# Eight expert token lists, 512-row matmul blocks, and output rows summed by gather and scatter in a linear-attention and mixture-of-experts kernel

## The chip, the cores and the metric

One NeuronCore of a Trainium2 chip. The metric is the device time of one execution in microseconds (us). The kernel before takes 836.64 us (median of 3 runs, 836.46 to 836.75). The engines are named as in the profile: PE is TensorE (PEld its weight loads), DVE is VectorE, ACT is ScalarE, POOL is GpSimd, SP is SyncE.

## The reference, cut to what matters

```python
def _attn_ref(q, k, v):                       # 8 batches, 8 heads, 576 tokens, 64 wide
    phi = lambda x: np.where(x > 0, x, np.exp(x) - 1.0) + 1.0
    kv  = np.einsum('bhsd,bhse->bhde', phi(k), v)
    num = np.einsum('bhsd,bhde->bhse', phi(q), kv)
    den = np.einsum('bhsd,bhd->bhs', phi(q), phi(k).sum(axis=2))[..., None] + 1e-06
    return num / den                          # 4608 token rows x of 512

def _moe_ref(x, w_gate, w_noise, noise, w1, w2):   # 8 experts, 512 -> 1024 -> 512
    noisy = x @ w_gate + np.log1p(np.exp(x @ w_noise)) * noise
    # the two largest per token and their softmax: top2, top2_w
    for e in range(8):
        for k in range(2):
            mask = top2[:, k] == e
            h = np.maximum(x[mask] @ w1[e], 0.0)
            out[mask] += top2_w[mask, k, None] * (h @ w2[e])
```

Every token goes through two experts, so 9216 rows run through the expert matmuls and every output row is the sum of two.

## The kernel before

Three stages follow one another. **Attention and routing** works through 40 tiles of up to 128 tokens. Each tile is routed by itself, with small VectorE operations on 128 x 8 elements, and scattered twice, into one sorted list per choice slot (first or second choice) and expert:

```python
    for b in range(B):
        # ... phi(q), phi(k), k-v products of the batch ...
        for ci in range(5):
            # ... numerator, division, logits, top 2, gates, positions of 128 tokens ...
            for sl in range(2):               # the row is multiplied by its gate here
                nc.vector.tensor_scalar(out=src[cs, sl, 0:HD]..., in0=xdiv_perm, scalar1=gk[cs], ...)
            for sl in range(2):
                nc.gpsimd.indirect_dma_start(
                    out=x_sorted[sl],
                    out_offset=bass.IndirectOffsetOnAxis(ap=pos_i[0:csz, sl : sl + 1], axis=0),
                    in_=src[0:csz, sl, :], in_offset=None)
```

**Experts**: 16 lists, padded to 768 rows (96 tiles of 128 rows). The first matmul runs in 128-column pieces. Its weights are read with a stride of eight columns (`fc::8`):

```python
        for fc in range(8):
            for dc in range(4):
                nc.tensor.matmul(
                    out=h_ps[:, fc, :],
                    lhsT=w1_sb[:, dc, fc::8],
                    rhs=xt_g[:, dc, tok0 : tok0 + P], ...)
        # ... Relu to bf16, eight 512-column matmuls into y_ps ...
        nc.vector.tensor_copy(out=y_sb[:], in_=y_ps[:])
        nc.gpsimd.indirect_dma_start(out=obig, out_offset=...orow_i[:, tt : tt + 1]..., in_=y_sb[:], ...)
```

**Last stage**: both halves of the output are read back, added and written (`phase_c`), 36 tiles.

## Time and profile before

| stretch of the span (832.2 us) | us | what bounds it |
|---|---|---|
| 0 to 54 | 54 | first q, k, v behind DMA |
| 54 to 359 | 305 | attention and routing, no engine full |
| 359 to 385 | 26 | last scatters, reading the sorted rows |
| 385 to 757 | 372 | expert matmuls, TensorE full |
| 757 to 833 | 76 | output halves read, added, written |

The stretches come from the rows of 40 slices, where each digit is a share in tenths over 20.8 us, and from the windows cut at the edges that they show. The lines themselves stand in the prediction below.

### The profile page before, as it was taken

What the parts mean: (1) busy time and instruction counts of PE and PEld (TensorE: products, weight loads), DVE (VectorE), ACT (ScalarE), POOL (GpSimd) and SP (SyncE); (2) the same over time, 40 slices, a digit from 0 to 9 for tenths busy, and PEclk for the clock granted to TensorE, in tenths of its full rate; (3) what the DMA queues carried; (4) which work ended last, traced back from release to release, by engine and by line L of the source; (5) the groups of instructions that cost most, each with busy time, mean ns of one, the idle gap of its engine ahead of it and who ended that gap; (6) DMA issues with size and microseconds to landing.
All of it is one profiled execution on the core that took longest, in us unless ns stands there. A gap on an engine that the chain in (4) does not pass through costs nothing.

```text
span 832.2 us, 13905 instructions
## 1 busy us (share of the span) xinstructions
PE 496.8 (60%) x5362; PEld 371.6 (45%) x5362; DVE 325.2 (39%) x1213; ACT 312.4 (38%) x514; POOL 309.7 (37%) x366
## 2 busy tenths in 40 slices
PE   0005253626345354306997979999999999993000
PEld 0004132415233243205775757777777777771000
DVE  3025555766758566631132231322323231112332
ACT  0027547768586766621322312232232322320000
POOL 5156674658475424320222212222222222222322
PEclk9999999999999999999998999999999999997555
DMA  9999997969596401159375291755643240104886
GB/s 294 249 197 91 279 190 72 79 78 99 65 106 70 60 21 47 52 140 152 128 127 209 57 270 50 126 224 95 254 83 65 68 86 33 39 33 140 288 276 231
DMA packets 212771, 108.69 MB, mean 131 GB/s; under 512 B 187616, under 2 KB 202976, under 8 KB 210656
## 3 DMA queue, kind: packets, MB, share of 16 engines
q0 software_dynamic: 124640, 45.69, 39.9%
q1 hardware_dynamic: 70336, 57.33, 27.2%
q10 hardware_dynamic: 17728, 4.77, 2.7%
q8 instruction: 42, 0.69, 0.3%
q14 instruction: 25, 0.20, 0.1%
HBM read 71.53 MB, written 37.81 MB: 131 GB/s over the span
## 4 chain that ended last, share of the span: by engine, by line
PE 41%; ACT 14%; issue 13%; DVE 8%; DMA 7%; POOL 3%; ACTq 0%; SPq 0%; POOLq 0%; DVEq 0%
PE h_ps L452 19%; PE y_ps L471 16%; ACT L306 5%; DMA out_big_s<-y_sb,orow_i 3%; PE kv_ps L210 2%; ACT L323 2%; POOL out_dram L528 2%; DVE phi_k L196 2%; ACT pqt_sb L233 2%; DVE src L353 1%; DMA x_sorted_s<-src,pos_i 1%; ACT xt_sb L292 1%; ACT L305 1%; PE nd_ps L251 1%; ACT L194 1%
## 5 line engine op out<-in xcount | busy, mean ns | idle before, releaser
L452 PEld LDWEIGHTS <-w_sb 128*128 128x128 bf16 x3072 | 208.6, 147 | 40.2 <-issue 22.7
L452 PE MATMUL h_ps<-xt_g,w_sb 128*128 128x128 bf16 x3072 | 208.9, 227 | 19.8 <-DMA xt_g<-x_sorted_s 19.8
L465 ACT ACTIVATE h_sb<-h_ps 128x512 bf16<-128x512 f32 x192 | 104.0, 595 | 290.1 <-PE h_ps L452 232.3
L479 POOL DMA_INDIRECT out_big_s<-y_sb,orow_i x96 | 95.1, 991 | 293.4 <-DVE y_sb L478 269.9
L471 PE MATMUL y_ps<-w_sb,h_sb 128*128 128x512 bf16 x768 | 184.8, 384 | 11.8 <-ACT h_sb L465 11.0
L478 DVE CAST y_sb<-y_ps 128x512 bf16<-128x512 f32 x96 | 65.6, 690 | 209.3 <-PE y_ps L471 208.3
L367 POOL DMA_INDIRECT x_sorted_s<-src,pos_i x80 | 85.5, 1069 | 115.4 <-DVE pos_i L341 59.4
L471 PEld LDWEIGHTS <-h_sb 128*128 128x128 bf16 x768 | 72.4, 100 | 82.7 <-ACT h_sb L465 12.0
L225 PE MATMUL pqt_psum<-ident,phi_q 128*128 128x128 bf16 (+1 forms) x160 | 26.4, 286 | 85.3 <-DVE phi_q L196 61.6
L225 PEld LDWEIGHTS <-phi_q 128*128 128x128 bf16 (+1 forms) x160 | 15.8, 121 | 92.1 <-DVE phi_q L196 62.9
L251 PE MATMUL nd_ps<-kv_sb,pqt_sb 64*128 64x64 bf16 (+1 forms) x320 | 38.4, 221 | 23.3 <-DVE xdiv L275 11.6
L306 ACT ACT_TABLE_LOAD x40 | 51.3, 1283 | 0.7
L210 PE MATMUL kv_ps<-v_ext,phi_k 128*64 128x65 bf16 (+1 forms) x320 | 33.0, 252 | 24.3 <-DVE phi_k L196 24.2
L194 ACT ACTIVATE escr<-q_nat 128x2048 bf16<-128x2048 bf16 (+1 forms) x16 | 20.3, 1269 | 69.9 <-DMA v_ext<-in_v_dram 51.5
L173 POOL DMA_DIRECT2D v_ext<-in_v_dram x40 | 35.5, 889 | 20.8 <-DMA q_nat<-in_q_dram 11.4
L527 DVE TENSOR_TENSOR o_t<-a_t,b_t 128x512 f32<-128x512 bf16 x36 | 24.6, 692 | 47.1 <-DMA b_t<-out_big_s 26.7
L169 POOL DMA_DIRECT2D k_nat<-in_k_dram x40 | 35.2, 881 | 20.9 <-DMA v_ext<-in_v_dram 9.7
L169 POOL DMA_DIRECT2D q_nat<-in_q_dram x40 | 36.1, 911 | 16.5 <-DMA k_nat<-in_k_dram 9.6
L353 DVE TENSOR_SCALAR src<-xdiv,g 128x512 bf16<-128x512 bf16 (+1 forms) x80 | 40.2, 514 | 0.0
L251 PEld LDWEIGHTS <-pqt_sb 64*128 64x128 bf16 (+1 forms) x320 | 28.4, 125 | 25.3 <-DVE xdiv L275 9.8
L528 POOL DMA_DIRECT2D out_dram<-o_t x36 | 19.6, 545 | 51.7 <-DVE o_t L527 51.5
L210 PEld LDWEIGHTS <-phi_k 128*64 128x64 bf16 (+1 forms) x320 | 23.8, 144 | 32.6 <-DVE phi_k L196 26.0
(73 smaller groups left out, 563.5 us busy)
## 6 DMA issues: line engine op xcount, KB each, us to landing
wstage<-in_moe_w_dram SPq DMA_DIRECT2D x16, 2048.0 KB
out_dram<-o_t POOLq DMA_DIRECT2D x36, 256.0 KB
x_sorted_s<-pad_row SPq DMA_DIRECT2D x16, 385.5 KB
a_t<-out_big_s SPq DMA_DIRECT2D x36, 128.0 KB
b_t<-out_big_s ACTq DMA_DIRECT2D x36, 128.0 KB
q_nat<-in_q_dram POOLq DMA_DIRECT2D x32, 128.0 KB
k_nat<-in_k_dram POOLq DMA_DIRECT2D x32, 128.0 KB
v_ext<-in_v_dram POOLq DMA_DIRECT2D x32, 128.0 KB
```

Source lines behind the costliest of these rows:

```text
L169: nc.gpsimd.dma_start(out=t_sb[0:csz, ci, :, :], in_=t_dram[b][:, s0 : s0 + csz, :].rearrange("h p d -> p h d"),)
L210: nc.tensor.matmul(out=kv_ps[par][po : po + 64, h // 2, :], lhsT=phi_k[0:csz, ci, h, :], rhs=v_ext[0:csz, ci, h, :], start=(h == par and c ...
L225: nc.tensor.matmul(out=pqt_psum[:, ci * P : ci * P + csz], lhsT=phi_q[0:csz, ci, 2 * hp : 2 * hp + 2, :], rhs=c["ident"][0:csz, 0:csz], is ...
L251: nc.tensor.matmul(out=num_v[par][0:csz, j, :], lhsT=lhsT, rhs=kv_sb[po : po + 64, j, 0:D], start=(j == 0), stop=False,)
L306: nc.scalar.activation(out=nsc[cs], in_=nsc[cs], func=ACT.Ln, bias=1.0, scale=1.0)
L353: nc.vector.tensor_scalar(out=src[cs, sl, 0:HD].rearrange("p (a b) -> p a b", a=4), in0=xdiv_perm, scalar1=gk[cs], scalar2=None, op0=ALU.mult)
L367: nc.gpsimd.indirect_dma_start(out=x_sorted[sl], out_offset=bass.IndirectOffsetOnAxis(ap=pos_i[0:csz, sl : sl + 1], axis=0), in_=src[0:csz ...
L452: nc.tensor.matmul(out=h_ps[:, fc, :], lhsT=w1_sb[:, dc, fc::8], rhs=xt_g[:, dc, tok0 : tok0 + P], start=(fc % 4 == 0 and dc == 0), stop=( ...
L465: nc.scalar.activation(out=h_sb[:, 4 * i : 4 * i + 4, :], in_=h_ps[:, 4 * i : 4 * i + 4, :], func=ACT.Relu,)
L471: nc.tensor.matmul(out=y_ps[:], lhsT=h_sb[:, fc, :], rhs=w2_sb[:, fc, :], start=(fc == 0), stop=(fc == 7),)
L478: nc.vector.tensor_copy(out=y_sb[:], in_=y_ps[:])
L479: nc.gpsimd.indirect_dma_start(out=obig, out_offset=bass.IndirectOffsetOnAxis(ap=orow_i[:, tt : tt + 1], axis=0), in_=y_sb[:], in_offset=None,
```

## The change

Its intent: eight lists, one per expert, padded to 1280 rows (80 tiles instead of 96); token blocks of 512 rows in the first matmul; the gate applied to the expert's output row, so the sorted rows carry the bare token; output rows written straight into the result, where the second expert of a token first gathers what the first one wrote; and the router run once for each of four groups of two batches. The diff, cut to its core:

```diff
-    for b in range(B):
-        ...                                   # 5 tiles a batch, each routed by itself
+    def run(self):
+        nxt = self.load(0)
+        for g in range(NG):                   # 4 groups of 2 batches, 9 chunks of 128 tokens
+            st = nxt
+            if g + 1 < NG:
+                nxt = self.load(g + 1)
+            ...phi, kv, transposes of q...
+            xrow, lwt = self.num(st, pqs, pqm, kvbds)
+            self.route(g, xrow, lwt)          # one routing for 1152 tokens, then 18 scatters
...
+        nc.vector.tensor_scalar_add(out=fld(0), in0=c["tokid"][:], scalar1=float(g * 2 * S))
...
-                    lhsT=w1_sb[:, dc, fc::8],
-                    rhs=xt_g[:, dc, tok0 : tok0 + P],
+                nc.tensor.matmul(out=ps[:, 0:n], lhsT=w1[:, dc, fc * P : fc * P + P], rhs=xt[:, dc, 0:n],
+                                 start=(dc == 0), stop=(dc == 3))       # n is 512, 512, 256
...
-        nc.vector.tensor_copy(out=y_sb[:], in_=y_ps[:])
+            nc.vector.scalar_tensor_tensor(out=y[:], in0=ps[:], scalar=gate, in1=L[:], op0=ALU.mult, op1=ALU.add)
+        r = nc.gpsimd.indirect_dma_start(
+            out=self.out, out_offset=bass.IndirectOffsetOnAxis(ap=si, axis=0),
+            in_=y[:], in_offset=None, bounds_check=N_TOK - 1, oob_is_err=False)
...
+                if t0 == 0:
+                    if e + 3 < E:
+                        self.load_w(e + 3)    # three weight buffers; cast to bf16 by the load
+                    for t in range(T_CAP):    # L: what earlier experts left in these rows
+                        L[t] = self.gather(gi[:, t : t + 1]) if e > 0 else None
...
-def phase_c(ctx, tc, out_big, out):
-    ...
```

## The prediction

> **What bounds the kernel now.** I read the 40 slices first, then the windows, the groups by line, and last the chain of waits. The slices show three stages that hardly overlap.
>
> ```profile
> PE   0005253626345354306997979999999999993000
> PEclk9999999999999999999998999999999999997555
> DMA  9999997969596401159375291755643240104886
> GB/s 294 249 197 91 279 190 72 79 78 99 65 106 70 60 21 47 52 140 152 128 127 209 57 270 50 126 224 95 254 83 65 68 86 33 39 33 140 288 276 231
> ```
>
> PE is nearly empty for the first 18 slices (20.8 us each), full from the 19th to the 36th, and empty at the end. The DMA engines are full in the first five slices and near full in the last three. I cut the span at these edges (columns: stretch, its us, then busy us and instructions of PE, PEld, DVE, ACT, POOL, then granted clock, DMA share, GB/s).
>
> ```profile
> 0.00:54.00 54.00, 0.33 (x2) 0.21 (x2) 6.28 (x15) 1.58 (x3) 19.00 (x52) 1.00 1.38 266
> 54.00:359.00 305.00, 132.62 (x1518) 98.03 (x1519) 189.00 (x948) 206.63 (x319) 171.67 (x180) 1.00 0.85 93
> 359.00:385.00 26.00, 4.89 (x37) 4.06 (x37) 6.02 (x29) 1.29 (x3) 4.25 (x3) 1.00 0.90 165
> 385.00:757.00 372.00, 358.96 (x3805) 269.29 (x3804) 99.33 (x188) 102.92 (x190) 94.45 (x96) 0.99 0.46 115
> 757.00:833.00 76.00, 0.00 (x0) 0.00 (x0) 24.58 (x36) 0.00 (x0) 20.29 (x37) 0.52 0.76 250
> ```
>
> So: 54 us of waiting for the first q, k and v behind DMA; 305 us of attention and routing in which no engine is full (ACT 206.6, DVE 189.0, POOL 171.7 busy), which is a chain of small steps with hand-overs, 40 tiles long; 26 us of draining the last scatters and reading x_sorted back; 372 us of expert matmuls, PE bound; 76 us in which the two halves of the output are read back, added and written, DMA bound. The groups that carry the change:
>
> ```profile
> L452 PE MATMUL h_ps<-xt_g,w_sb 128*128 128x128 bf16 x3072 | 208.9, 227 | 19.8 <-DMA xt_g<-x_sorted_s 19.8
> ...
> L479 POOL DMA_INDIRECT out_big_s<-y_sb,orow_i x96 | 95.1, 991 | 293.4 <-DVE y_sb L478 269.9
> L471 PE MATMUL y_ps<-w_sb,h_sb 128*128 128x512 bf16 x768 | 184.8, 384 | 11.8 <-ACT h_sb L465 11.0
> L478 DVE CAST y_sb<-y_ps 128x512 bf16<-128x512 f32 x96 | 65.6, 690 | 209.3 <-PE y_ps L471 208.3
> L367 POOL DMA_INDIRECT x_sorted_s<-src,pos_i x80 | 85.5, 1069 | 115.4 <-DVE pos_i L341 59.4
> ...
> L306 ACT ACT_TABLE_LOAD x40 | 51.3, 1283 | 0.7
> ```
>
> The mean of a pipelined matmul is not its price, so the price comes from the chain of waits (start, us, what):
>
> ```profile
> 390.24 1.96 PE h_ps L452 x32
> 392.20 1.73 PE y_ps L471 x8
> ...
> 436.29 7.77 DMA out_big_s<-y_sb,orow_i
> ...
> 756.73 3.37 DMA out_big_s<-y_sb,orow_i
> ```
>
> Thirty-two 128-column matmuls cost 1.97 us (61.6 ns each), eight 512-column ones 1.73 us (216 ns each). The same scatter takes 3.4 us from issue to landing at the quiet end, and 7.8 us beside a weight load.
>
> [...] the trace has 81 loads of 1283 ns, 104 us in all. [...] The 7.8 us scatter above shared engines with a load on another queue; no run yet shows one behind a load on its own queue, which the change creates.
>
> **Expert matmuls.** Before, 16 lists padded to 768 rows are 96 tiles of 32 x 61.6 ns + 8 x 216 ns = 3.70 us, 355 us, plus some 16 us of stalls at the first three expert boundaries. After, 8 lists padded to 1280 rows are 80 tiles. By the seed the reference routes 1110 to 1185 rows to each expert, so nothing overflows and the slow path is skipped. One expert's first matmul is two 512-row blocks of 32 x 216 ns and one 256-row block of 32 x 109 ns, 17.3 us; its second is 80 x 216 ns, 17.3 us. 34.6 us x 8 = **277 us**, 78 less: 59 of it from 16 fewer tiles[...]. ACT is no bound: 0.595 us per 0.86 us chain. DVE gets about 0.69 us for the gated eviction[...]. POOL gets a scatter and a gather a tile, 2 x 1.27 us (0.96 plus the 0.3 gap between issues), plus 4 weight loads: some 28 of 34.6 us.
>
> **The last stage** goes: 76 us. What stays is one last eviction, a scatter (3.4 us) and the test for overflow, about 9 us.
>
> **The new wait.** The gather of expert e+1 must wait until every scatter of expert e has landed. From the last second-matmul of e, PE can still do the first matmul of block 1 (6.9 us) and three output tiles (5.2 us), 12 us in all, before its three output buffers are full. The path beside it: eviction 0.7, scatter issue and landing 3.4, gather issue and landing 3.4, addition 0.7, hand-overs about 0.5: 9 us, hidden. But for the first five boundaries a weight buffer comes free at that moment, and 2.1 MB of w2 go onto the same software queue ahead of the scatter: 7 us at the 290 GB/s of the first slice. Then it is 16 us or more, and the traffic of one such expert (4.2 MB weights, 1.3 rows in, 2.6 out, about 1.2 gathered, 9.3 MB in 34.6 us, 270 GB/s) is close to all that this trace ever moves. I take 7 us a boundary, **35 us**[...]. Experts: 320 us.
>
> **Attention and routing.** Four groups of two batches in place of eight batches and 40 tiles. Work per group, from the rows of before. ACT: four 2048-wide Exp at 1.9, two 512-wide at 0.63, PSUM copies 6.2, table loads 3 x 1.28: about 20 us. DVE: relu+1 four times 0.73 and min eight times an estimated 0.69, tails 2, masks 2, nine chunks of 1.3 (0.69 for 512 PSUM elements, 0.3 for 128 and two of 0.16), and about 34 small routing operations of 0.2[...]: about 33 us. POOL: 12 loads of 0.8 and 18 scatters of 1.27: 33 us. So 4 x 33 = 135 us if it streams. Loads come as 1 KB pieces in place of 256 B and the initial fill falls from 6.2 to 2.2 MB, so work starts near 12 us, not 54. But three experts' weights (12.6 MB) now share the software queue with the q, k, v loads (28.3 MB): with fill and scatters some 53 MB, 190 us at 280 GB/s. I expect DMA, not DVE, to pace this stage, with the last group routed near 188 us. Then 18 scatters of 1.27 us follow with nothing to cover them, 23 us, and landing, transposed read and first matmuls: PE full at about **212 us** against 385.
>
> Sum: 212 + 320 + 9 = 541 us of span; before, the span was 4.4 us under the measured time, so about **545 us**.
>
> **Rivals.** (1) The weights get in the way at the start: the scheduler puts them ahead of the later q, k, v loads. For it: [...] slices 1 to 5 are already full. It would move the handover to 235 us and the end to 570. (2) POOL becomes the bound of the expert stage: bounds-checked indirect DMAs may cost more than 0.96 us, which no row here prices. At 1.6 us plus the gap, 20 of them and the loads make 41 us an expert, 50 us in all: about 590. (3) Everything hides: no DMA pacing (handover 185) and no boundary wait (experts 285): about 485. Against it speaks the near-full DMA. (4) The gain vanishes because the scatter-gather chain serialises tiles; against it, the gathers are needed once per expert, not per tile, so even 25 us at each of seven boundaries leaves 685 us, still far below 837.
>
> **Range and chances.** The handover lies within 185 to 240, the expert stage within 285 to 345, both tied to the same DMA load, so 490 to 600. Only a chain serialised at every tile could lose 290 us: chances 0.98, 0.01, 0.01.
>
> **What would show it.** Right: windows with PE first full near 212; 34.6 us of PE per expert; gaps before the fourth output tile at the first five boundaries, ended by a gather and absent at the last two; no DMA-only stage at the end. Wrong: PE waiting for POOL all through the experts (rival 2), evictions waiting on gathers in the middle of an expert, a DMA row far from full before the handover, or the first Exp starting after 25 us.

Where passages are marked as cut, they told of the hardware what no trace or run of this case shows, or gave an estimate without what it was worked out from. The 81 loads of 1283 ns are ScalarE's table loads, and the 7.8 us scatter (436.29 us) ran in a window where the DMA share was 1.00 and 376 GB/s moved, 2.77 of 2.92 MB on the queue of the weight load. The sum of the prediction was 212 + 320 + 9 = 541 us. Its 320 are 277 + 35 and a term of 8 us for a slow start of the experts, which is cut; without it the sum would be 533 us. Cut too are a term of 1.3 us in the 33 us of VectorE per group (that reduction took 2.07 us in the changed kernel), VectorE's estimate for clearing L (0.485 us there, the gated eviction 0.731), and the reason for 19 of the 78 us less.

Three of its inputs were first measured in the changed kernel. Thirty-two 256-column matmuls took 3.49 us (274.62 to 278.11 us), 109 ns each. The load packets took 60 ns for 512 B (2 to 30 us), where the kernel before took 32 ns for 128 B (2 to 54 us; medians; 512 and 128 B are what the 1 KB and 256 B pieces leave in bf16). The first Exp began at 15.75 us (12 predicted; 53.86 in the kernel before).

## The result, and the profile after

The changed kernel takes 595.71 us (median of 4 runs, 592.61 to 600.70), and its result is correct. Before, beside it: 836.55 us. The ratio is 0.7145 (95% interval 0.7099 to 0.7191). In the experiments below, ratios are the mean time of a version's timed runs over that of the kernel before in the same rounds, so not quite the ratio of the medians; the profiled first run of each is not in them. (On one core a run is labelled slow by a rule of 1.5% alone. Two runs of the pipelined version and two of the control are so labelled at an unchanged clock. Their reported ratios agree with all three timed rounds, so I count those runs. The one timed run of each that is labelled fast would give 0.6735 for the pipelined version and 0.7095 for the control, so differences of under 1% against these two are not firm.)

The rows of 40 slices, 14.9 us each, of the changed kernel:

```profile
PE   0173173137245300199989928969948968989984
PEclk9996555556555555589999978998987998998998
DMA  9999954995602002555864993993893995573153
GB/s 168 210 191 191 191 131 101 192 209 157 124 27 102 36 10 106 128 91 130 184 101 121 184 110 80 228 140 101 217 120 101 243 146 145 189 157 145 57 160 128
```

TensorE works in bursts up to the 14th slice, hardly at all in the next three, and is nearly full from the 18th on; the last stage is gone. The DMA row is full in the first five slices and again in the 8th and 9th, and nearly empty from the 12th to the 16th: 10 to 106 GB/s move there. The clock row stands at half for nearly the whole routing stage, at a granted clock of 0.50 to 0.54 in the windows below, where the attention stage of the kernel before had 1.00. What the half clock costs this stage no run here isolates.

The windows, cut where a group of two batches begins its 18 scatters (74.7, 130.3, 174.1 and 221.2 us in the timeline; columns: stretch, its us, busy us and instructions of PE, PEld, DVE, ACT, POOL, granted clock, DMA share, GB/s), with the expert stage last:

```profile
74.00:130.00 56.00, 20.96 (x146) 13.65 (x146) 28.88 (x100) 17.19 (x18) 32.24 (x34) 0.50 0.88 155
130.00:174.00 44.00, 20.11 (x145) 12.93 (x144) 26.56 (x89) 12.53 (x14) 20.73 (x20) 0.54 0.50 114
174.00:221.00 47.00, 18.38 (x132) 12.05 (x129) 20.32 (x83) 8.82 (x12) 17.43 (x18) 0.50 0.14 52
221.00:251.00 30.00, 0.00 (x0) 0.00 (x0) 4.68 (x20) 0.00 (x0) 17.32 (x18) 0.50 0.37 106
...
251.10:587.60 336.50, 292.77 (x1408) 141.83 (x1408) 95.51 (x210) 99.41 (x192) 163.89 (x168) 0.93 0.69 145
```

In each of the periods of 56, 44 and 47 us no engine works much more than half the time, and in two of them DMA doesn't either. So this is a chain again, not a bound. The first expert matmul starts at 251.1 us (212 predicted), the experts take 336.5 us (320 predicted), and 7.8 us follow (9 predicted).

The costliest groups (busy us, mean ns of one; then idle time just before and what ended most of it):

```profile
L474 PE MATMUL h_ps<-xt,w 128*128 128x512 bf16 (+1 forms) x768 | 150.5, 355 | 39.5 <-DMA xt<-x_sorted 32.3
...
L483 PE MATMUL y_ps<-w,hT 128*128 128x512 bf16 x640 | 149.8, 392 | 36.5 <-DVE y L489 36.5
L490 POOL DMA_INDIRECT out_dram<-y,si x80 | 79.4, 992 | 97.4 <-DVE y L487 39.9
...
L376 POOL DMA_INDIRECT x_sorted<-xrow,posi x72 | 73.6, 1022 | 78.9 <-DVE xrow L373 33.7
L461 POOL DMA_INDIRECT L<-out_dram,gi x70 | 70.6, 1009 | 82.1 <-DMA out_dram<-y,si 60.6
```

Scatter and gather with the bounds check cost 0.99 and 1.01 us of GpSimd each, plus the gap of 0.3: rival 2 (1.6 us) is out. The waits that matter (engine and line, released by; us in total, times, longest):

```profile
POOL L L461 <- DMA out_dram<-y,si: 60.6, 6, 16.1
...
PE kv_ps L335 <- DVE A L331: 44.2, 4, 16.4
...
PE y_ps L483 <- DVE y L489: 36.5, 6, 12.9
...
ACT e L185 <- DMA qm<-in_q_dram: 18.2, 2, 16.9
```

The first is the new wait: a gather of the next expert waits until the last scatters of this one have landed. The third is what TensorE sees of it. The second is what I did not foresee: TensorE stands at the routing matmul of a group, and the k-v products of the next group stand behind that matmul. In seven traces (this one and those of r_after, e_shift, a3_wlate, b1_wmid, b2_nogather and b4_noreload) TensorE runs the same 1976 matmuls in one order, whatever they wait for; this is what I call an in-order queue. The fourth is a link of the same kind: the last q rows of group 3 are issued only at 104.2 us, behind the 18 scatters of group 0 in GpSimd's queue. ScalarE (97.0 to 113.9 us) and VectorE (104.3 to 113.9 us) wait for them, with work of group 1 behind.

The chain of waits around the boundary at 490 us, and in a full stretch later:

```profile
473.96 8.41 DMA out_dram<-y,si
...
488.27 3.30 DMA L<-out_dram,gi
...
492.46 3.48 PE y_ps L483 x8
...
546.80 6.91 PE h_ps L474 x32
```

A scatter beside a weight load takes 8.41 us to land, the gather after it 3.30. Thirty-two 512-column matmuls take 6.91 us, 216 ns each, as predicted. But eight of them straight after the wait took 3.48 us, not 1.73: the granted clock was 0.50 from 488.9 to 495.7 us (5.75 us of idle time before them). The four longest gaps of this trace between expert matmuls (5.33 to 12.87 us) all end so, with eight matmuls of 3.48 to 3.57 us in the timeline. After the gaps of 1.72 and 0.68 us eight took 1.89 us there, at a granted clock of 1.00.

### The profile page after: what moved, and what is told of

Its sections match the earlier page's. It is cut to its first block, busy times and chain, and to the rows that moved or that the text cites. A ratio compares the mean times of both kernels' runs of the same rounds, so it can differ in the third digit from the quotient of the medians. Undisturbed runs are those within 1.5% of the kernel's fastest.

```text
span 595.4 us, 5833 instructions
## 1 busy us (share of the span) xinstructions
PE 373.5 (63%) x1976; PEld 194.5 (33%) x1976; DVE 221.8 (37%) x638; ACT 170.2 (29%) x265; POOL 288.7 (48%) x315
## 5 line engine op out<-in xcount | busy, mean ns | idle before, releaser
L474 PE MATMUL h_ps<-xt,w 128*128 128x512 bf16 (+1 forms) x768 | 150.5, 355 | 39.5 <-DMA xt<-x_sorted 32.3
L476 ACT ACTIVATE hT<-h_ps 128x512 bf16<-128x512 f32 (+1 forms) x192 | 99.4, 527 | 260.8 <-PE h_ps L474 209.2
L483 PE MATMUL y_ps<-w,hT 128*128 128x512 bf16 x640 | 149.8, 392 | 36.5 <-DVE y L489 36.5
L490 POOL DMA_INDIRECT out_dram<-y,si x80 | 79.4, 992 | 97.4 <-DVE y L487 39.9
L474 PEld LDWEIGHTS <-w 128*128 128x128 bf16 x768 | 77.8, 101 | 111.1 <-issue 46.9
L376 POOL DMA_INDIRECT x_sorted<-xrow,posi x72 | 73.6, 1022 | 78.9 <-DVE xrow L373 33.7
L461 POOL DMA_INDIRECT L<-out_dram,gi x70 | 70.6, 1009 | 82.1 <-DMA out_dram<-y,si 60.6
L483 PEld LDWEIGHTS <-hT 128*128 128x128 bf16 x640 | 64.1, 100 | 115.5 <-issue 45.3
L489 DVE SCALAR_TENSOR_TENSOR y<-y_ps,gate,L 128x512 f32<-128x512 f32 x70 | 51.1, 731 | 98.8 <-PE y_ps L483 60.6
L460 DVE MEMSET L<- 128x512 f32 x70 | 34.0, 485 | 34.4 <-DMA x_sorted<-xrow,posi 24.4
L270 PE MATMUL num_ps<-kvbd,pqt 128*128 128x162 bf16 x128 | 22.2, 324 | 38.6 <-DVE lwt L293 34.6
L335 PE MATMUL kv_ps<-A,ut 128*128 128x72 bf16 x4 | 0.9, 219 | 44.2 <-DVE A L331 44.2
```

The costliest lines, as they stand in the source:

```text
L270: nc.tensor.matmul(out=ps[:, hp, 0:KVW], lhsT=pqs[j][:, hp, cc * P : cc * P + P], rhs=kvbds[j][:, hp, :], start=(hp % 2 == 0), stop=(hp % ...
L376: r = nc.gpsimd.indirect_dma_start(out=self.x_sorted, out_offset=bass.IndirectOffsetOnAxis(ap=posi[:, ci, sl : sl + 1], axis=0), in_=xrow[ ...
L460: nc.vector.memset(L[:], 0.0)
L461: nc.gpsimd.indirect_dma_start(out=L[:].bitcast(INT32), out_offset=None, in_=self.out.bitcast(INT32), in_offset=bass.IndirectOffsetOnAxis( ...
L474: nc.tensor.matmul(out=ps[:, 0:n], lhsT=w1[:, dc, fc * P : fc * P + P], rhs=xt[:, dc, 0:n], start=(dc == 0), stop=(dc == 3))
L476: nc.scalar.activation(out=hT[:, fc, 0:n], in_=ps[:, 0:n], func=ACT.Relu)
```

## The experiments

All on one core. From the trace of each version I read three times: the handover (start of the first expert matmul), the experts (from there to the end of the last), and the gaps (all gaps over 0.4 us between expert matmuls, summed).

| version | handover us | experts us | gaps us | median us | ratio to before |
|---|---|---|---|---|---|
| changed kernel | 251.1 | 336.5 | 43.7 | 595.71 | 0.7145 |
| the same again (r_after) | 251.0 | 325.3 | 35.4 | 595.24 | 0.7151 |
| unused tile (e_shift) | 236.9 | 340.0 | 50.5 | 587.33 | 0.7035 |
| token number tied (a1_tokid) | 231.9 | 338.2 | 49.4 | 583.56 | 0.7005 |
| next group's products first (a2_pipe) | 208.4 | 328.3 | 38.3 | 564.04 | 0.6778 |
| weights after routing (a3_wlate) | 254.7 | 354.8 | 65.8 | 622.25 | 0.7453 |
| weights in mid-expert (b1_wmid) | 237.7 | 316.9 | 26.2 | 564.71 | 0.6777 |
| no gathers, wrong result (b2_nogather) | 253.5 | 281.3 | 1.1 | 545.00 | 0.6524 |
| no weight reloads, wrong result (b4_noreload) | 238.0 | 279.9 | 0.5 | 533.65 | 0.6400 |
| 128-column pieces (d_mm128) | 252.5 | 350.5 | 40.4 | 611.06 | 0.7314 |
| combined (c_all) | 213.7 | 306.8 | 19.6 | 532.28 | 0.6388 |
| combined, weights after scatters (c2_wtie) | 213.3 | 312.3 | 24.8 | 533.15 | 0.6388 |
| combined, weights two ahead (c3_wnext) | 219.0 | 317.4 | 28.0 | 552.25 | 0.6581 |

The traces are of single runs; those of r_after and a2_pipe are of their fastest (586.11 and 556.08 us), so their stages add up to less than the median.

### Does DMA pace the routing stage? (a3_wlate)

```diff
-        for e in range(3):
-            pb.load_w(e)              # emitted inside the attention stage
     with ExitStack() as bctx:
         pb.open(bctx)
+        for e in range(3):
+            pb.load_w(e)
```

Their three buffers are allocated there too.

> Edit: the weights of the first three experts (12.6 MB) are not loaded during attention and routing but only after it. The step of my prediction under test: 'I expect DMA, not DVE, to pace this stage.' If DMA paces it, a quarter of its bytes gone must move the last scatter issue from 243 us to 200 or earlier. My theory now (a serial chain through in-order queues paces it): the last scatter issue stays within 235 to 245 us, the DMA row is even emptier, and the experts start 5 to 15 us later, since their first weights then come after the last scatters: time 600 to 615 us, ratio 0.72 to 0.735.

The last scatter was issued at 230.4 us, not at 242.8. But part of the 242.8 is a hold that this version does not have (next experiment): without it the unedited stage issues its last scatter at 228.7 us. A quarter of the bytes gone thus moved nothing (+1.7 us). DMA does not pace the stage after the first group's scatters (from 74.7 us on), and rival 1 (the weights get in the way at the start) is out. Of the first 75 us, in which the DMA row is full, this run says nothing: in the changed kernel too the first weight load is issued only at 104.9 us. The experts then pay for the late weights: 354.8 us, and the ratio of 0.745 lies above what I expected.

### A hold that comes and goes (r_after, e_shift)

The control has no edit. The other has one unused tile:

```diff
     c["carry"] = carry
+    unused = consts.tile([P, NG, NC], FP32, name="unused")
+    nc.vector.memset(unused[:], 0.0)
```

> Control: the changed kernel unedited, a second time. In its first trace the fourth group of the routing stage took 47 us, with about 10 us (190 to 199.5 us) in which TensorE's completions came late for no reason that the trace shows; in two runs whose routing stage is the same program (weights moved in mid-expert, weights late) that group took 34 and 37 us. If this hold belongs to the one trace, the fourth period is near 34 us here, the handover near 238 us and the time near 582; if it belongs to the kernel, the handover is again near 251 and the ratio again near 0.7145.

> Edit: one unused constant tile of 144 bytes per partition and its memset, which moves the later tiles in memory and changes nothing else. In all four traces with the routing stage unedited (the changed kernel twice, 128-column pieces, no gathers) the fourth group took 47 us with TensorE's completions late between 184 and 199.5 us; in the three with the stage or its loads edited it took 34 to 37 us. If the hold is an accident of addresses, it is gone here: fourth period about 34 us, handover about 238 us, time about 582. If it belongs to the schedule of this stage, nothing changes: handover 251 us, ratio 0.71 to 0.72.

The control repeats the handover within 0.1 us, and its fourth period, 47 us, too: the hold belongs to this build of the kernel. With the unused tile it is gone: the period is 33.8 us (173.5 to 207.3) and the handover 236.9 us. This is the timeline of ScalarE in the changed kernel (start, us, what, idle before and its releaser):

```profile
188.28 1.01 ACT L248 COPY pqt<-t_ps 128x1024 bf16<-128x1024 bf16 x1 [2.77 <-PE t_ps L244]
199.49 1.93 ACT L248 COPY pqt<-t_ps 128x1024 bf16<-128x1024 bf16 x2 [10.19 <-remote]
```

and this the same place with the unused tile:

```profile
182.23 1.01 ACT L250 COPY pqt<-t_ps 128x1024 bf16<-128x1024 bf16 x1 [5.55 <-PE t_ps L246]
183.14 0.59 ACT L227 COPY kvt<-t_ps 128x512 bf16<-128x512 bf16 x1
183.94 2.84 ACT L250 COPY pqt<-t_ps 128x1024 bf16<-128x1024 bf16 x3 [0.21 <-PE t_ps L246]
```

Three copies of transposed queries run back to back below, and are 11 us apart above. In the held build the last transposes had been issued to TensorE by 190.4 us and signalled their end only near 199.5 us. The hold stands in four traces of three builds (changed kernel and control, d_mm128, b2_nogather) and is missing in b1_wmid, b4_noreload and a3_wlate, which do not edit the routing code either. TensorE's queue up to there holds the same instructions in the same order in the control and in b1_wmid, and the fetches of instructions fall alike in both traces. So it is worth 14 us and is not part of the schedule. Its cause stays open.

The time fell by only 8 to 10 us of these 14 (by the medians and by the ratios). In the same four unedited expert stages (changed kernel, control, e_shift, a1_tokid) the experts took 325 to 340 us and their gaps 35 to 50 us. Why these waits differ so much from trace to trace is open, too. It is 2.5% of the time, and smaller differences between versions I do not explain.

### In-order queues in the routing stage (a1_tokid, a2_pipe)

In the changed kernel the token number of group g+2 goes into the tile from which group g is still being scattered. The write stands early in VectorE's queue, and waits there:

```profile
101.40 0.18 DVE L362 TENSOR_SCALAR xrow<-tokid 128x9 f32<-128x9 f32 x1 [5.26 <-issue]
```

a1_tokid makes the write depend on its own group's routing code, so that it cannot stand early:

```diff
-        nc.vector.tensor_scalar_add(out=fld(0), in0=c["tokid"][:], scalar1=float(g * 2 * S))
+        nc.vector.scalar_tensor_tensor(out=fld(0), in0=code[:, 0], scalar=0.0, in1=c["tokg"][:, g],
+                                       op0=ALU.mult, op1=ALU.add)
```

> Edit: the token number of a group is written with a value that depends on this group's own routing code, so the write can no longer stand early in VectorE's queue and wait there for the 18 scatters of the group before last. In the changed kernel two such waits were 5.3 and 4.8 us. My theory (the first stage is a serial chain through the engines' in-order queues, of which this head-of-line wait is one link): these two waits go, the handover to the experts comes 5 to 10 us earlier (about 243 us instead of 251), the experts do not change, the time falls by 5 to 10 us, ratio to before about 0.705. Rival (DMA or POOL's scatters pace the stage): the two waits go, others grow by as much, handover unchanged at 251.

The handover is at 231.9 us, 19 earlier than in the changed kernel and, fairly compared, 5 earlier than in the build without the hold. That is the low end of the 5 to 10 us expected for this one link, and the trace shows why. Of the two waits (5.3 and 4.8 us) the first was swallowed: VectorE went on to the late q rows at once and waited there 14.6 us instead of 9.6, and the first period stayed at 54.5 us (55.1 in the build without the hold). Only the second period fell, from 43.3 to 36.9 us. The ratio, 0.7005, is a little below the expected 0.705, because the hold went along with it, partly given back in the experts.

a2_pipe emits the next group's work in front of this group's routing (and gives the transposed queries a fourth buffer):

```diff
+        ready = prep(nxt)                     # phi, kv, q transposes of group 0
+        nxt = self.load(1)
         for g in range(NG):
-            ...phi, kv, transposes of group g...
+            st, pqs, pqm, kvbds = ready
             xrow, lwt = self.num(st, pqs, pqm, kvbds)
+            if g + 1 < NG:
+                ready = prep(nxt)
             self.route(g, xrow, lwt)
```

> Edit: the phi, k-v products and q transposes of group g+1 are emitted before the routing of group g, so that TensorE's queue has work in front of the routing matmul. In the changed kernel TensorE stood 44.2 us in four waits in front of that matmul (line 335), and the groups followed each other at 56, 44 and 47 us. My theory (the in-order queue of TensorE serialises the groups): the waits at the routing matmul fall from 44 to below 15 us, the periods fall to 33 to 38 us, the last scatter issue moves from 243 to about 205 to 215 us, PE is full near 215 to 222, time falls by 25 to 35 us, ratio about 0.66 to 0.68. Rival (VectorE's own work, about 27 us busy a group, plus the scatters' landing pace it): periods stay above 44 us and the time falls by less than 10 us.

TensorE's wait at the routing matmul fell from 44.2 to 11.2 us:

```profile
PE kv_ps L335 <- DVE A L331: 11.2, 3, 9.1
```

The periods are 40, 32 and 23 us, and the handover is 208.4 us, 28.5 us before the build without the hold. The serial chain is thus the largest part of the missing time, and the rival (VectorE's own work) is out. But not all of it is TensorE's queue: the edit also emits the loads of the group after next before this group's scatters. All but one of the last q, k and v loads are now issued by 75.8 us, and the wait of 9.6 us for the late q rows is gone with the others. No run parts the two. The end of this run holds something else: GpSimd's closing drain took 8.0 us (7.9 in c3_wnext, 0.9 to 5.2 in the others). I did not find out why.

### What makes the boundary wait? (b2_nogather, b4_noreload, b1_wmid)

```diff
 b2:  -  L[t] = self.gather(gi[:, t : t + 1]) if e > 0 else None
      +  L[t] = self.gather(gi[:, t : t + 1]) if e > 99 else None
 b4:  -  self.load_w(e + 3)
      +  self.w[e + 3] = self.w[e]
```

> Edit, with a wrong result on purpose: no expert gathers the first half of its output rows, so no expert waits for the scatters of the one before it, and the second scatter of a row overwrites the first. This bounds what the new scatter to gather wait costs. My theory: the boundary waits (36.5 us) vanish with the cold clock that follows them; experts about 285 to 292 us instead of 336, close to the 277 of TensorE work; ratio about 0.655 to 0.665. Rival (the gaps at the boundaries are due to the weight loads on the scatters' queue, not to the gather): gaps of over 15 us remain.

> Edit, with a wrong result on purpose: no expert's weights are loaded after the first three (experts 3 to 7 compute with the weights of 0 to 4, which are not yet given up), so the scatter to gather chain at the boundaries has no weight traffic beside it. My prediction's step: without a weight load the chain is about 9 us and hidden behind 12 us of TensorE work; the load makes it longer at the first five boundaries. If right: boundary gaps sum to under 5 us, experts about 281 to 290 us (the version without gathers took 281.3), ratio 0.65 to 0.665. Rival (the chain alone is longer than what TensorE has beside it): gaps of 15 us or more remain and the experts take over 300 us.

Both empty the gaps (1.1 and 0.5 us). Without gathers the experts take 281.3 us, without weight reloads 279.9 us. In the latter GpSimd's wait for landed scatters is

```profile
POOL L L461 <- DMA out_dram<-y,si: 7.1, 3, 2.5
```

instead of 60.6 us. So the chain of scatter and gather alone is hidden behind TensorE, as predicted; it is the weight load beside it that makes it long. Whether the shared queue or the shared DMA engines do this is not parted: in the kernel before, the weights were loaded on SyncE's queue, and the scatter beside such a load (436.29 us) still took 7.77 us. The rivals of both runs (gaps without gathers; gaps without loads) are out. The experts lose 45 to 57 us to this pair (325.3 and 336.5 against 279.9).

b1_wmid keeps the loads but moves them: a fourth buffer, filled in mid-expert.

```diff
-                if t0 == 0:
-                    if e + 3 < E:
-                        self.load_w(e + 3)
+                if t0 == 4 and e + 3 < E:
+                    self.load_w(e + 3, y)     # tied to a row block y that is already evicted
```

> Edit: a fourth weight buffer, and the weights of expert e+3 issued in the middle of expert e rather than at the boundary, where they stood on the same queue between the last scatters and the gathers that wait for them. In the changed kernel the waits before the second matmul at the boundaries sum to 36.5 us, 12.9 us the longest, and the two boundaries without a weight load had none. My theory (the weight load in the queue delays the scatter to gather chain): the boundary waits sum to less than 8 us, the experts take about 300 to 308 us instead of 336, ratio 0.675 to 0.685; the first stage does not change. Rival (the chain of scatter, landing, gather and landing itself is longer than the 12 us of work that TensorE has beside it): the waits stay above 20 us. A second rival: weight traffic in the middle delays the scatters there and evictions wait for gathers later: the waits only move, in sum as long as before.

Gaps of 26 us, experts 316.9 us: better, but only by half of what I expected. (The ratio, 0.6777, lies in the expected range by luck, since the hold of 14 us is missing here.) GpSimd's timeline shows why the experts gained so little:

```profile
308.37 1.55 POOL L433 DMA_DIRECT2D w<-in_moe_w_dram  x2
...
317.56 0.97 POOL L496 DMA_INDIRECT out_dram<-y,si  x1 [0.76 <-DVE gate L447]
329.46 1.04 POOL L467 DMA_INDIRECT L<-out_dram,gi  x1 [10.93 <-DMA out_dram<-y,si]
```

The load is issued at 308 us, the last scatter at 317.6 us, and the gather still waits 10.9 us. Mid-expert is too late. That the 4.2 MB are still moving when the boundary comes is my reading of this wait. The second rival (the waits only move) holds in part. The later combined version issues the loads right after the gathers.

### What the block size is worth (d_mm128)

```diff
-            for dc in range(4):
-                nc.tensor.matmul(out=ps[:, 0:n], ..., rhs=xt[:, dc, 0:n], ...)
+            for t in range(n // P):
+                for dc in range(4):
+                    nc.tensor.matmul(out=ps[:, t * P : t * P + P], ..., rhs=xt[:, dc, t * P : t * P + P], ...)
```

> Edit: only the block size is undone: the first expert matmul runs as 128-column pieces again, four for each 512-column one (the results are the same). My prediction's step: thirty-two 128-column matmuls cost 1.97 us against 1.73 us for the same rows as eight 512-column ones, so 80 tiles cost 80 x 0.24 = 19 us more TensorE time, and since TensorE is the bound between boundaries, most of it shows, less what the boundary waits absorb: time up by 12 to 20 us, ratio 0.73 to 0.74. Rival (the 512-row blocks matter through fewer instructions or shorter waits[...]; or the boundary waits swallow it): up by less than 6 us.

The time is 15.8 us above the control on the same chip, inside the expected 12 to 20 (13.6 us by the ratios; the control's own runs span 586 to 601 us, so the size is rough). The step behind it is nevertheless wrong. The chain of waits of this version has

```profile
285.99 7.15 PE h_ps L475 x128
```

128 matmuls of 128 columns in 7.15 us are 55.9 ns each, not 61.6. The pieces add 80 x 32 x (55.9 - 54.0) ns = 5 us. The other 11 us are not in the price of a matmul in such a full stretch. The group view of this version shows more idle time before the first matmul's pieces than the changed kernel has there (3.9 us for ScalarE and 3.3 without a recorded cause):

```profile
L475 PE MATMUL h_ps<-xt,w 128*128 128x128 bf16 x2560 | 159.5, 225 | 61.5 <-DMA xt<-x_sorted 32.2 <-issue 17.6 <-ACT hT L479 11.5
```

In return its waits before the second matmul are shorter (13.9 us, against 36.5 in the changed kernel and 27.2 in the control), so the sum of its gaps, 40.4 us, lies between those two (43.7 and 35.4). What is left shows in the spacing of the matmuls: those at about double price cost 19 us extra here, 13 in the changed kernel and 10 in the control. In these single traces, part of what the larger blocks save is thus time in matmuls at double price (the granted clock of the expert stage is 0.93 here and in the changed kernel, 0.95 in the control). What causes the idle time under "issue" stays open.

### Versions meant to beat both (c_all, c2_wtie, c3_wnext)

c_all joins a1_tokid, a2_pipe and a fourth weight buffer whose load is tied to a gathered tile, and issues the noise loads from SyncE instead of ScalarE:

```diff
                     for t in range(T_CAP):
                         L[t] = self.gather(gi[:, t : t + 1]) if e > 0 else None
+                    if 0 < e < E - 3:
+                        self.load_w(e + 3, L[3])
```

> A version meant to beat both: the pipelined routing stage and the token number tied to its group together, noise loads moved off ScalarE's queue, and a fourth weight buffer whose loads are issued right after the gathers of each expert (tied to the landing of the fourth gather) rather than in its middle. Expected by my theory: handover near 200 to 205 us (208 with the pipelining alone), experts 300 to 308 us (317 with the load in mid-expert), tail 8 to 10: span 510 to 525, time 512 to 527, ratio 0.615 to 0.63. If the savings do not add (the scatters of the routing stage, 23 us a group, become its pace; or the weight loads delay evictions), the time stays above 540.

532.28 us, correct: 11% under the changed kernel on the same chip (0.6388 to 0.7151), and 36% under the kernel before. It missed my range by 5 us because the handover came at 213.7 us. Its GpSimd timeline shows the new bound of the stage:

```profile
139.94 0.96 POOL L381 DMA_INDIRECT x_sorted<-xrow,posi  x1 [1.61 <-DMA w<-in_moe_w_dram]
...
180.28 0.96 POOL L381 DMA_INDIRECT x_sorted<-xrow,posi  x1 [0.30 <-issue]
181.54 0.96 POOL L381 DMA_INDIRECT x_sorted<-xrow,posi  x1 [0.31 <-issue]
```

From 158.7 to 203.0 us the scatters of the last two groups follow each other at 1.27 us with no wait: GpSimd is full, and before that eight of them stood behind weight loads. c2_wtie and c3_wnext try to clear these: the first three loads go behind the scatters of groups 1, 2 and 3 (c2); only two are loaded there, and from then on expert e loads e+2 (c3).

```diff
             self.route(g, xrow, lwt)
+            if g > 0:                         # c3: if g in (1, 2)
+                self.pb.load_w(g - 1, self.f0)
```

> Edit on the combined version: the weights of experts 0, 1 and 2 are issued after the scatters of groups 1, 2 and 3, where the DMA engines are nearly idle, and no longer ahead of the scatters of groups 0 and 1. In the combined version GpSimd issues the last 36 scatters back to back, and the eight scatters from 125 to 142 us took 2.6 us each instead of 1.27, waiting for weight loads. My theory (GpSimd's scatters now pace the routing stage): the 10 us of these waits go and the handover moves from 213.7 to 202 to 208 us; time 522 to 530 us, ratio 0.625 to 0.635. Rival (the weights arrive late: the first experts then wait for them): time not below 532 us.

> Edit on the combined version, after the last run: only two experts' weights are loaded during routing (after the scatters of groups 1 and 2), and from then on the weights of expert e+2, not e+3, are issued in expert e, right after its gathers; three weight buffers are enough. In the last run the last scatter was issued at 195.8 us instead of 203.0, but the first expert matmul stayed at 213.3 us: my reading is that the third load, issued right behind the last scatters, delayed their landing and the transposed read. If so, the handover is now 8 to 10 us after the last scatter, at 202 to 206 us, experts 305 to 312 us as before, time 518 to 526 us, ratio 0.62 to 0.632. If the reading is wrong, the handover stays near 213 us and the ratio at 0.639; if weights two experts ahead come too late, gaps before the first matmul of an expert appear.

Both miss. In c2_wtie the last scatter was issued at 195.8 us (203.0 in c_all), but the first expert matmul stayed at 213.3 us. I put this down to the third load behind the scatters; c3_wnext took that load away, and its handover came later still (last scatter at 210.6, first matmul at 219.0 us), at 552.25 us in all. The 8 us from last scatter to first matmul came out as expected there, the rest did not: TensorE waited 5.3 us for the small VectorE copies that tie the weights, and the closing drain cost 7.9 us again. The reading of c2_wtie is not settled. c_all and c2_wtie are equal within their intervals, and c_all is the simpler.

## Why the prediction was right or wrong, point by point

- **Faster, inside the range**: 595.71 us against 545 (490 to 600). The sum is 50 us too small. That the time lies inside is partly luck: it is 4 us from the edge, one of the four runs (600.70) is outside, and the handover at 251.1 us is outside its own range of 185 to 240.
- **Handover at 212 us: wrong by 39 us.** The step that failed is "I expect DMA, not DVE, to pace this stage, with the last group routed near 188 us." The last group's scatters began at 221 us with DMA nearly idle (the prediction's own sign of being wrong, "a DMA row far from full before the handover", came true), and a3_wlate shows that DMA does not pace it after the first group. In its place stand: a serial chain through in-order queues (28.5 us, a2_pipe against e_shift: TensorE's queue, and up to some 10 us of it the late q rows in GpSimd's; VectorE's early write, 5 us by a1_tokid, is a further link of such a kind and still waited 4.3 us once in a2_pipe), and 14 us of hold. Together 42.7 us: with the order mended the handover is at 208.4. That this is near the predicted 212 is luck: DMA, which was to set that pace, was busy for 0.71, 0.80 and 0.29 of the three periods of a2_pipe. The costs were not at fault where the trace can be compared (VectorE's minimum of 1024 elements took 684 ns, estimated 0.69 us; the reduction of the cut term is an exception). The prediction summed each engine's work per group and left out in which order the queues hold it.
- **Scatters with nothing to cover them, 23 us**: right, 221.2 to 242.8 us for the 17 intervals between 18 issues.
- **Experts, 277 us of TensorE work**: right. 34.6 us for each expert is what the 6.91 us pieces make, and b4_noreload took 279.9 us. The first 64 matmuls of the changed kernel took 16.75 us, against 13.8 at 216 ns each; the granted clock was 0.50 from 251.1 to 256.7 us and 1.00 from 256.8 to 267.5. So the slow start cost 2.9 us there, where the cut term put 8.
- **78 us less, 59 of them from fewer tiles**: right, and the other 19 us too: the price fell from 61.6 to 54 ns per 128 columns of the first matmul. The reason given for these 19 us came from no trace; 128-column matmuls run at 55.9 ns in d_mm128. Among other things the weight read differs from before: the weight loads of the first matmul took 147 ns with the stride in the kernel before, and 101 and 100 ns without it in the changed kernel and in d_mm128 (means of the groups by line). No run isolates it, so the cause of the 61.6 ns was not shown.
- **The new wait, 35 us**: right in mechanism and place (first five boundaries, absent at the last two), right in cause (gaps of 1.1 us in b2_nogather, 0.5 us in b4_noreload). Its size was 36.5 us in the changed kernel, 27.2 in the control. Added to it is what I left out, the matmuls at a granted clock of 0.50 after the longer gaps (3.48 to 3.57 us for eight after 5.33 to 12.87 us); together 45 to 57 us of expert time against the 35 predicted.
- **Last stage gone, 9 us left**: right, 7.8 us.
- **Rivals.** Rival 1 (weights in the way of the loads) and rival 2 (indirect DMAs dearer) are out. Rival 3 (everything hides, about 485 us) did not happen; the fastest version, c_all, took 532 us. Rival 4 (a chain at every tile) is out; the chain was there once per group and once per expert.

## What to carry to other kernels

Summing each engine's work per step was not enough here (handover 212 us predicted, 251.1 measured): look at what stands in front of the next step's work in each engine's queue. The routing matmuls held TensorE for 44.2 us in four waits in the changed kernel, and for 11.2 us in a2_pipe, which puts other work before them. Where a scatter must land before a gather can start, keep large loads away from them at that moment (a scatter took 8.41 us to land beside a weight load in the changed kernel, 3.37 at the quiet end of the kernel before), and issue them right after the gathers (gaps of 19.6 us in c_all, 43.7 in the changed kernel). And when a kernel shows a wait of 10 us that its own order cannot explain, rebuild it with a harmless change before explaining it: one unused tile removed the hold of 14 us here.
